# The folded weight of an mLSTM and feed-forward kernel by seven half-block products a row pair, its sums on GpSimd, and quarter products split in two

## The chip, the cores and the metric

One core of one Trainium2 chip. The metric is the device time of one launch in microseconds, as the median of several runs of the same kernel; the profile is one more execution, with the hardware profiler on. TensorE is called PE, VectorE DVE, ScalarE ACT, GpSimd POOL and SyncE SP, as the profile does.

## The reference

An mLSTM cell for 4 batches, 8 heads, 768 time steps and head width 40, then a feed-forward part whose two hidden products are multiplied. Cut to what matters here:

```python
# cell, for each time step t:
C = f_stab * C + i_stab * outer(v[t], k[t]);  n = f_stab * n + i_stab * k[t]
y[t] = sigmoid(o_gate[t]) * (C @ q[t]) / max(abs(n @ q[t]), 1)
# feed-forward: x is y with the 8 heads side by side, 3072 tokens x 320
a = x @ w1                  # 320 -> 1024
b = x @ w2                  # 320 -> 1024
h = a * b @ w3              # 1024 -> 1024
out = h @ w_out             # 1024 -> 320
```

All arrays are float32 (w1, w2, w3 and w_out arrive as float64 and are converted by the kernel). Since `(a * b @ w3) @ w_out` is `(a * b) @ (w3 @ w_out)`, the kernel computes the product `w3 @ w_out`, 1024 x 320, once and calls it w3o. This is "the fold".

## The kernel before, in words

**Blocks and steps.** The tokens are 24 blocks of 128 (6 stretches of time by 4 batches). A Python loop over s writes the whole program out, 32 steps long; nothing loops on the chip. Step s computes the cell of block s and finishes the output y of block s - 1 (`quarter_work`, from L338). Around the cell, each step has pieces of the feed-forward part:

- `up`: for 256 tokens and two of the eight blocks f of 128 hidden columns, the products x·w1 (tile pa) and x·w2 (pb). The 320 rows of x are two times 128 and a rest of 64; the rest is done by "quarter products" of 64 x 64 x 256, four of which share the array (`up_rest`, L631). `up_rest` then copies pa to a_sb on ACT (L638) and multiplies pb by a_sb on DVE into ab (L639). One up block runs in each of steps 2 to 5, two in each of steps 6 to 15.
- `fetch`, `scale_next`, `convert` (L211 to L251): a piece of a weight is read by SP, scaled on ACT (L191, L195) and turned into float32 on DVE (L199, L200). Pieces of w3 are also transposed on DVE, in squares of 32 (L248), into tiles w3T: two buffers, one for each row block ko of 128 of the 1024 rows. n_cvt says how many pieces step s converts; the reads run four pieces ahead.
- `fold`, `w3_mm` (L253 to L264): a row block whose w3T is ready costs eight products of 128 x 128 x 320 into a bank wp, one for each 128 of the 1024 inner terms (ki), which ACT then copies into w3o (L264). Two row blocks are folded in step 10, one in each of steps 11 to 16.
- `ffn_out` (L733): ab times w3o into a bank po, copied to o_sb on ACT (L741) and written out; from step 16.
- Steps 19 to 30 have `up_by_seven` and steps 27 to 31 `out_by_seven`, which do the same work on larger blocks by seven products of half blocks for eight (Strassen's scheme in Winograd's form), with the sums by `weight_sums`, `token_sums`, `out_weight_sums` and `ab_sums` on POOL and DVE.

**The cell on the engines.** PE: products of the weights and of the state (ph, pi), then of q and k (ss) and of the decayed v and k (pc). DVE: h (L423, L430), the masked product of the scores (L397), the state (L404, L414), the denominator (L438 to L441), the gated output (L443, L445), then the turned copies of k and q for the next step (L317, from step 9), and after them the converts. POOL: the decayed state (L335), which waits for L404; vw of the next block (L330); two masks (L308); and until step 16 a copy that doubles y's rest (L476).

**What sets the order.** Each engine works through its own list in the order in which the program writes the operations; PE's order is pinned by `in_order` (L84), and `issue_after` puts chosen operations behind others on the same list (the converts stand behind the turn of the next q and k, L967). Semaphores carry the rest. PE writes into four rotating banks of PSUM for px (y transposed), wp, pa, pb and po; the cell has four banks of its own. `x_trans` (L486) turns y of an earlier block to xT by PE and a copy on ACT.

Of the kernel before, what the change touches and what calls it, by code (L numbers as in the profile page):

```python
# [8 lines left out]
FP = mybir.dt.float32  # L9
# [7 lines left out]
def kernel(  # L17
# [59 lines left out]
    def mps(shape, name):  # L77
        pool = banks.pop(0)
        banks.append(pool)
        return pool.tile(shape, FP, name=name, tag="m")  # L80
# [10 lines left out]
    def mm(out, lhsT, rhs, start=True, stop=True):  # L91
        in_order(nc.tensor.matmul(out, lhsT=lhsT, rhs=rhs, start=start, stop=stop))  # L92
# [135 lines left out]


    w3T_t = {}  # L230
    turned_w3, ready_w3 = [], []

    def scale_next(early=False):
        scaled.append(pend.pop(0))
# [2 lines left out]
    def convert():  # L237
        if not scaled:
            scale_next()
        dst, raw, ko, half = scaled.pop(0)  # L240
        if dst is not None:
            to_f32(dst, raw)
            return
        w3 = wst.tile([128, CW], FP, name="w3", tag="w3")
        to_f32(w3, raw)
        if half == 0:
            w3T_t[ko] = wst.tile([128, FO, 128], FP, name="w3T", tag="w3T")
        nc.vector.transpose(out=w3T_t[ko].rearrange("c k (m r) -> c m k r", r=32)[:, 2 * half:2 * half + 2],  # L248
                            in_=w3.rearrange("r (m c k) -> r m k c", m=2, k=FO))
        if half:  # L250
            turned_w3.append(ko)  # L251

    def fold():  # L253
        while ready_w3:
            w3_mm(ready_w3.pop(0))
        ready_w3.extend(turned_w3)
        turned_w3.clear()

    def w3_mm(ko):
        w3T = w3T_t.pop(ko)  # L260
        wp = mps([128, DM], "wp")
        for ki in range(FO):
            mm(wp, w3T[:, ki, :], wo[:, ki, :], start=(ki == 0), stop=(ki == FO - 1))
        nc.scalar.mul(out=w3o[:, ko, :], in_=wp, mul=UP ** -2)  # L264


    qT_t, kT_t, vw_t, before_t, y_t, x_t = {}, {}, {}, {}, {}, {}
# [65 lines left out]
    def decayed(new, old, n, x):  # L333
        c, b = divmod(n, B)
        nc.gpsimd.tensor_tensor(out=new, in0=old, op=OP.mult, in1=decay[:, b * NP:(b + 1) * NP, 2 * c + x:2 * c + x + 1]  # L335
                                .to_broadcast([P, NP, D1]))
# [281 lines left out]
    def up(gr, fs, cs):  # L618


        if gr not in ab_t:
            ab_t[gr] = [ffn.tile([128, FO, 2 * P], FP, name="ab", tag="ab", bufs=6) for _ in range(2)]
        x, n = x_t[gr], cs.stop - cs.start
        pa, pb = mps([128, len(fs), n], "pa"), mps([128, len(fs), n], "pb")
        for p, wt in ((pa, w1), (pb, w2)):
            for i, f in enumerate(fs):
                for cc in range(KF):
                    mm(p[:, i, :], wt[:, cc, f * 128:(f + 1) * 128], x[:, cc, cs], start=(i == cc == 0), stop=False)
        return pa, pb, x, gr, fs, cs

    def up_rest(pa, pb, x, gr, fs, cs):  # L631
        for i, f in enumerate(fs):
            for j, e in quarters:
                mm((pa, pb)[j][halves[e], i, :], wr[halves[j], f * 128 + e * L:f * 128 + (e + 1) * L],
                   x[halves[j], KF, cs], start=False, stop=(i == len(fs) - 1))
        j, t0 = divmod(cs.start, 2 * P)
        a_sb = ffn.tile([128, len(fs), cs.stop - cs.start], FP, name="a_sb", tag="a_sb")
        nc.scalar.mul(out=a_sb, in_=pa, mul=UP ** -2)  # L638
        nc.vector.tensor_tensor(out=ab_t[gr][j][:, fs[0]:fs[-1] + 1, t0:t0 + a_sb.shape[-1]], in0=pb, in1=a_sb, op=OP.mult)  # L639

# [87 lines left out]

        return single, shared, left, product

    def ffn_out(blocks, pos=None):  # L733

        pos = pos or [mps([P, DM], "po") for _ in blocks]
        for (gr, j), po in zip(blocks, pos):
            for f in range(FO):
                mm(po, ab_t[gr][j // 2][:, f, j % 2 * P:(j % 2 + 1) * P], w3o[:, f, :], start=(f == 0), stop=(f == FO - 1))
        for (gr, j), po in zip(blocks, pos):
            o_sb = ffn.tile([P, DM], FP, name="o_sb", tag="o_sb", bufs=2)  # L740
            nc.scalar.copy(out=o_sb, in_=po)  # L741
            t0 = j * S + gr * P
            nc.scalar.dma_start(out=out[t0:t0 + P, :], in_=o_sb)


    KH, NH = FO // 2, DM // 2

    def out_weight_sums():

        T_o.extend(m[:, i * KH * NH:(i + 1) * KH * NH].rearrange("p (f n) -> p f n", n=NH)  # L750
                   for m, i in ((v_all, 0), (gates, 0), (gates, 1), (q_all, 0)))
        (B11, B12), (B21, B22) = ([w3o[:, k * KH:(k + 1) * KH, i * NH:(i + 1) * NH] for i in range(2)] for k in range(2))
        T1, T2, T3, T4 = T_o
        for dst, p, q in ((T1, B12, B11), (T2, B22, T1), (T3, B22, B12), (T4, B21, T2)):
            yield nc.gpsimd.tensor_tensor(out=dst, in0=p, in1=q, op=OP.subtract)

    T_o, S_o = [], {}
    wsums = out_weight_sums()

    def quarters_of_ab(gr, j):  # L760
        return [[ab_t[gr][j][:, k * KH:(k + 1) * KH, t * P:(t + 1) * P] for k in range(2)] for t in range(2)]
# [49 lines left out]
    n_out = [0] * 27 + [1, 0, 1, 0, 3]  # L811
    w12 = [("w12", i, part) for part in range(2) for i in range(2 * KF + 1)]
    todo = w12[5:] + [("wo", i, 0) for i in range(FO)] + [("w3", ko, part) for ko in range(FO) for part in range(2)]
    n_cvt = [0, 0, 2, 0, 1, 2, 3, 3, 3] + [2] * 6
    n_fetch = [5, 5, 10]
    pinned, ahead = 32, 9
    behind = ExitStack()
# [2 lines left out]
    for s in range(len(n_up)):  # L820
# [21 lines left out]
        if s < NU:  # L842
            if s >= B:
                decayed(state[s % B][1], state[s % B][0], s, 0)
        if s == 2 or N_DVE < s < NY + 2:
            twice(s - 2)
        if NY <= s - 2 < NU:
            get_back(s - 2)
        while s >= N_DVE and turned < min(s - 2, NY):
            x_trans(turned)  # L850
            turned += 1
        fold()
        if s >= len(n_up) - 2:
            ab_sums(*summed.pop(0))
        def pairs():
# [13 lines left out]
            seven[1]()  # L869
        if seven and s <= NU:  # L870
            ffn_out([downs.pop(0) for _ in range(n_down[s])], [cell[1][:, i, 0:DM] for i in range(2)])
        else:
            for _ in range(n_down[s]):
                ffn_out([downs.pop(0)])
# [2 lines left out]
        if seven and s > NU:  # L877
            seven[0]()
        now = [ups.pop(0) for _ in range(n_up[s])]
        open_ups = [up(*x) for x in now] if s != 2 else []  # L880
        if s == 3:
            turn(3)
        def rest():
            for x in open_ups:
                up_rest(*x)
            if seven:
                seven[2]()
            if s == 3:
                scale_next()
                scale_next()  # L890

        def between():
            twice(1)
            weighted(2)
            rows_of_u(3)
            for _ in range(3):
                scale_next()
            for n in range(2):
                x_trans(n)
                if n == 0:  # L900
                    warm(1, small=38)
            for _ in range(3):
                convert()
            turn(2)
            block = up(*now[0])
            weighted(3)
            weights(3)
            masks(3)
            out_gate(2)
            convert()  # L910
            up_rest(*block)

        gated = None
        if s <= NU:
            gated = quarter_work(s, rest, between if s == 2 else None, convert if s == 3 else None)
        else:
            rest()
        with tc.issue_after(gated.ins) if gated else nullcontext():
            if seven:
                seven[3]()  # L920
            for _ in range({NU: 1, NU + 1: 3}.get(s, 0)):
                next(wsums)
            if s == NU + 1:
                ab_sums(*summed.pop(0))
            if NY <= s - 2 < NU:
                x_turn(s - 2)
            for n in () if s == 1 else (s + 2,) if s < B else (s + 2, s + 3) if s == B else (s + 3,):
                if n < N_U:
                    rows_of_u(n)
            if N_DVE <= s + 1 < NU:  # L930
                gated = turn(s + 1)
            if s - 2 in range(4 * GT - 1, NU, GT):
                token_sums((s - 2) // GT)
            if s < len(n_up) - 2 and n_out[s + 1] and s > NU + 2:
                ab_sums(*summed.pop(0))
# [28 lines left out]
        if s == B:  # L964
            for i, r in enumerate(third):
                nc.sync.dma_start(out=U_d[i * GC:(i + 1) * GC].rearrange("c r t -> r c t"), in_=U3[r])
        with tc.issue_after(gated.ins) if N_DVE <= s + 1 < NU else nullcontext():  # L967
            for _ in range(n_cvt[s] if s < len(n_cvt) else 0):
                convert()
                converted += 1  # L970
# [9 lines left out]
            for ins in keep_order(front):  # L980
                behind.enter_context(tc.issue_after(ins))
    behind.close()
    assert not ups and not sevens and not downs and not outs and not summed and not todo and not pend and not turned_w3 and not ready_w3, (len(ups), len(downs), len(todo), len(pend))
# [1 line left out]
_INS = ['q', 'k', 'v', 'i_gate', 'f_gate', 'o_gate', 'moe_w1', 'moe_w2', 'moe_w3', 'moe_w_out']  # L985
_OUTS = [((3072, 320), 'float32')]
# [25 lines left out]
```

## Time and profile before

| what | value |
|---|---|
| runs of the kernel before | 426.22, 426.43, 430.01 us; median 426.43 |
| the profiled execution | 427.89 us, its span 425.8 us |
| granted PE clock, mean | 0.996 |
| PE busy | 414.1 us, 97% of the span |
| DVE busy | 313.5 us, 74% |
| POOL busy | 154.3 us, 36% |
| ACT busy | 150.1 us, 35% |
| DMA, share of the 16 engines in hardware queues | 53.9% and 2.7% |
| products of the fold (wp) | 128 records, 35.9 us busy |
| POOL, subtraction of 128 x 512 (L711) | 27.4 us in 22, 1268 ns each |
| POOL, subtraction of 128 x 640 (L755) | 4, of 1545 to 1995 ns |
| DVE, product ab of two PSUM and SBUF inputs (L639) | 16.4 us in 24, 688 ns each |

A row of the groups of instructions reads: line, engine, operation, output <- inputs, shapes, count, then busy time and mean of one, then the idle time of the engine just before them and what ended it. A float32 product is two records on PE (and two weight loads on PEld). Records overlap in PE's pipeline, so the mean of one is longer than the distance from one to the next. In the chain of waits, "issue" is time in which the engine waited for nothing that the profile shows.

### The profile page before, as it was taken

Reading aid. Unit: us, or ns where it says so; the run is one execution under the profiler, and the core shown is the slowest. Engines: PE = TensorE matmul, PEld = TensorE weight load, DVE = VectorE, ACT = ScalarE, POOL = GpSimd, SP = SyncE. Lnnn points to the kernel's source line nnn. Section 1 sums busy time; section 2 is a strip of 40 time slices with the busy share of each in tenths; the row PEclk is TensorE's granted clock in tenths of the full one; section 3 lists DMA queues with packets and bytes.
Section 4 is the critical chain, followed back from the end, with each engine's and each line's share of the span. In section 5 each row is a group of like instructions: output and inputs, shape, how many; then the busy total and the mean of one; then the engine's idle time right before and its main releaser. Section 6 shows DMA issues by size and latency. Waiting matters only on the chain.

```text
span 425.8 us, 13079 instructions
## 1 busy us (share of the span) xinstructions
PE 414.1 (97%) x5353; PEld 335.3 (79%) x5353; DVE 313.5 (74%) x635; ACT 150.1 (35%) x404; POOL 154.3 (36%) x211
## 2 busy tenths in 40 slices
PE   7989989999999999999999999999999999999996
PEld 4768878888688788787777778788778879888896
DVE  6676986888949779778736966596868699575971
ACT  4766865567723623630433313032311110210000
POOL 4421342233303303303307751546453587542100
PEclk9989999999999999999999999999999999999999
DMA  8999998598977776985425675756421120000001
GB/s 186 204 173 245 214 144 140 134 193 180 215 183 154 166 182 135 181 164 105 89 80 130 153 141 121 142 133 117 87 44 36 35 39 2 31 2 31 2 32 62
DMA packets 135211, 51.15 MB, mean 120 GB/s; under 512 B 109360, under 2 KB 126960, under 8 KB 135152
## 3 DMA queue, kind: packets, MB, share of 16 engines
q1 hardware_dynamic: 131552, 46.29, 53.9%
q10 hardware_dynamic: 3600, 4.03, 2.7%
q8 instruction: 42, 0.69, 0.7%
q14 instruction: 17, 0.14, 0.1%
HBM read 44.50 MB, written 5.80 MB: 118 GB/s over the span
## 4 chain that ended last, share of the span: by engine, by line
PE 53%; issue 20%; DVE 7%; POOL 7%; SPq 7%; DMA 5%; ACT 1%; POOLq 0%; DVEq 0%
PE cell L92 17%; PE pa L92 12%; PE o L92 8%; PE pb L92 8%; PE p L92 3%; POOL pw L308 3%; SPq L184 3%; DVE w3T L666 2%; PE pt L95 1%; POOL vw L330 1%; SPq L148 1%; DMA raw<-in_moe_w_dram 1%; PE fill L92 1%; POOL raw L659 1%; POOL state L335 1%
## 5 line engine op out<-in xcount | busy, mean ns | idle before, releaser
L335 POOL TENSOR_TENSOR state<-state,decay 128x164 f32<-128x164 f32 x40 | 20.0, 500 | 154.8 <-DVE state L404 129.0
L92 PE MATMUL pa<-xT,w 128*128 128x256 f32 x240 | 60.4, 382 | 0.0
L92 PEld LDWEIGHTS pa<-xT,w 128*128 128x128 f32 x240 | 44.4, 190 | 6.8 <-DVE h L430 0.4
L303 ACT ACTIVATE pw<-pw,aT 128x64 f32<-128x64 f32 x184 | 46.4, 339 | 3.2 <-ACT o_sb L741 1.9
L92 PE MATMUL pb<-xT,w 128*128 128x256 f32 x192 | 45.4, 379 | 0.0
L729 POOL TENSOR_TENSOR ab<-ab,a_sb 128x512 f32<-128x512 f32 x22 | 29.4, 1356 | 32.2 <-DVE ab L684 32.2
L92 PEld LDWEIGHTS pb<-xT,w 128*128 128x128 f32 x192 | 36.4, 190 | 5.0
L711 POOL TENSOR_TENSOR wo<-wo 128x512 f32<-128x512 f32 x22 | 27.4, 1268 | 29.8 <-DVE wo L686 29.8
L92 PE MATMUL pa<-xT,wr 64*64 64x256 f32 x384 | 37.0, 386 | 0.5 <-DVE wr L200 0.5
L92 PE MATMUL wp<-wo,w3T 128*128 128x320 f32 x128 | 35.9, 433 | 1.1 <-DVE ab L639 0.6
L308 POOL TENSOR_SCALAR_AFFINE_SELECT pw<-pw 64x512 f32<-64x512 f32 x48 | 35.8, 746 | 3.0 <-ACT pw L303 1.2
L92 PE MATMUL pb<-xT,wr 64*64 64x256 f32 x384 | 36.4, 380 | 0.0
L92 PE MATMUL cell<-w3o,ab 128*128 128x320 f32 x128 | 35.4, 432 | 0.0
L638 ACT ACTIVATE a_sb<-pa 128x512 f32<-128x512 f32 x24 | 14.3, 598 | 59.0 <-PE pb L92 59.0
L639 DVE TENSOR_TENSOR ab<-pb,a_sb 128x512 f32<-128x512 f32 x24 | 16.4, 688 | 23.2 <-ACT a_sb L638 22.8
L92 PEld LDWEIGHTS wp<-wo,w3T 128*128 128x128 f32 x128 | 23.8, 190 | 10.5 <-DVE ab L639 0.8
L92 PEld LDWEIGHTS cell<-w3o,ab 128*128 128x128 f32 x128 | 24.3, 190 | 9.5
L92 PEld LDWEIGHTS pa<-xT,wr 64*64 64x64 f32 x384 | 18.9, 132 | 15.4 <-issue 8.8
L686 DVE SCALAR_TENSOR_TENSOR a_sb<-pa,wo 128x512 f32<-128x512 f32 x12 | 8.3, 689 | 29.8 <-PE pa L92 29.8
L430 DVE TENSOR_TENSOR h<-cell,h 64x164 f32<-64x164 f32 x88 | 28.6, 326 | 1.6
L92 PE MATMUL po<-w3o,ab 128*128 128x320 f32 x96 | 26.4, 433 | 0.0
L92 PEld LDWEIGHTS po<-w3o,ab 128*128 128x128 f32 x96 | 18.1, 190 | 7.3
(180 smaller groups left out, 846.4 us busy)
## 6 DMA issues: line engine op xcount, KB each, us to landing
raw<-in_moe_w_dram SPq DMA_DIRECT2D x64, 128.0 KB, 3.4
kbuf<-in_k_dram SPq DMA_DIRECT2D x24, 160.0 KB, 4.5
v_all<-in_v_dram SPq DMA_DIRECT2D x24, 160.0 KB, 4.9
o_in<-in_o_gate_dram SPq DMA_DIRECT2D x24, 160.0 KB, 4.8
pw<-U_d SPq DMA_DIRECT2D x28, 128.0 KB, 3.5
raw<-in_moe_w_dram SPq DMA_DIRECT2D x5, 512.0 KB, 6.7
raw<-in_moe_w_out_dram SPq DMA_DIRECT2D x8, 320.0 KB, 4.1
gates<-in_k_dram SPq DMA_DIRECT2D x28, 80.0 KB, 2.5
```

The source lines that it names most:

```text
L92: in_order(nc.tensor.matmul(out, lhsT=lhsT, rhs=rhs, start=start, stop=stop))
L184: nc.sync.dma_start(out=dst, in_=src)
L303: nc.scalar.activation(out=pw[:, h, :], in_=src[:, h, :], func=AF.Exp, bias=aT[:, c, b * H + h:b * H + h + 1])
L308: nc.gpsimd.affine_select(out=pw[r], in_=pw[r], compare_op=OP.is_ge, fill=0.0, base=0, pattern=[[0, H], [1, L]], channel_multiplier=-1)
L335: nc.gpsimd.tensor_tensor(out=new, in0=old, op=OP.mult, in1=decay[:, b * NP:(b + 1) * NP, 2 * c + x:2 * c + x + 1] .to_broadcast([P, NP, D1]))
L430: nc.vector.tensor_tensor(out=part, in0=ph[x][halves[e]], in1=part, op=OP.add)
L638: nc.scalar.mul(out=a_sb, in_=pa, mul=UP ** -2)
L639: nc.vector.tensor_tensor(out=ab_t[gr][j][:, fs[0]:fs[-1] + 1, t0:t0 + a_sb.shape[-1]], in0=pb, in1=a_sb, op=OP.mult)
L666: nc.vector.tensor_tensor(out=dst, in0=p, in1=q, op=OP.subtract)
L686: nc.vector.scalar_tensor_tensor(out=out, in0=p, scalar=UP ** -2, in1=q, op0=OP.mult, op1=OP.add)
L711: aside_by.tensor_tensor(out=kept[j][:, 1:4:2], in0=kept[j][:, 1:3], in1=kept[j][:, 3:4].to_broadcast([128, 2, TH]), op=OP.add)
L729: aside_by.tensor_tensor(out=t[:, f:FO:FH, :], in0=t[:, f:FO:FH, :], in1=a, op=OP.mult)
```

## The change

1. **The fold.** The eight row blocks of w3 are taken as four row pairs (i). With A the 256 x 1024 pair, cut in 2 x 2 blocks (by row block and by half of the inner terms), and B = w_out cut in 2 x 2 (half of the inner terms, half of the 320 columns), the pair's 256 x 320 result takes seven products of half blocks instead of eight, each of four matmuls of 128 x 128 x 160: 28 of width 160 in place of 16 of width 320. Sums are S1 = A21 + A22, S2 = S1 - A11, S3 = A11 - A21, S4 = A12 - S2 and T1 = B12 - B11, T2 = B22 - T1, T3 = B22 - B12, T4 = B21 - T2.
   - `fold_first`: A11·B11 and A12·B21 into wp (8 matmuls), copied on ACT by `first_copy`. At the end of steps 9, 11, 13 and 14, behind the cell.
   - `fold_second`: A22·T4, S1·T1, S2·T2, S4·B22, S3·T3 into wq and wp (20 matmuls), copied on ACT to M2 and M1. In steps 10, 12 and 14 between the first up block (with its quarter products) and the second; in step 16 between the first six and the last two f of `ffn_out` (with the cell ahead of those last two).
   - its five adds (three of 160 columns, two of 320): on POOL behind the cell in steps 10, 12, 14, on DVE in step 16.
   - the T sums on POOL: T1 and T2 in step 8; T4 and T3 (in B12's place) in step 9, ahead of and behind the S sums. The S sums (four of 128 x 512) on POOL in steps 9, 11, 13, 15. S3 takes A21's place in w3T; B21 - T2 is formed once more in step 15 for the last pair, in B21's place, since the last pair's result takes the place in w3o where T4 lay.
   - memory: S and M in a spare ab tile or spare raw tiles; T in a new tile fold_m and in w3o; o_sb lives in fold_m; the w3 tile has one buffer for two.
2. **Two steps' piece counts.** n_cvt is 3 for 2 in step 5 and 2 for 3 in step 8: a piece of w_out comes a step earlier, and the fetches with it.
3. **Copies and products.** In steps 9, 11 and 13 both a_sb copies are written ahead of both products ab; in these steps `x_trans` stands at the end of the step.
4. **Split quarter products.** In steps 2, 3 and 4 (both f) and in step 6 (first up block, first f) a quarter product of 64 x 64 x 256 is written as two of 64 x 64 x 128.

The diff, cut to its core:

```diff
-    def w3_mm(ko):
-        w3T = w3T_t.pop(ko)
-        wp = mps([128, DM], "wp")
-        for ki in range(FO):
-            mm(wp, w3T[:, ki, :], wo[:, ki, :], start=(ki == 0), stop=(ki == FO - 1))
-        nc.scalar.mul(out=w3o[:, ko, :], in_=wp, mul=UP ** -2)
...
+    def fold_weight_sums():
+        (B11, B12), (B21, B22) = halves_of(wo)
+        T1, T2, T4 = (m.rearrange("p (f n) -> p f n", n=NH) for m in
+                      (fold_m[:, 0], fold_m[:, 1], w3o[:, FO - 2:FO].rearrange("p k n -> p (k n)")))
+        fold_T.extend((T1, T2, B12, T4))
+        for dst, p, q in ((T1, B12, B11), (T2, B22, T1), (T4, B21, T2), (B12, B22, B12)):
+            yield nc.gpsimd.tensor_tensor(out=dst, in0=p, in1=q, op=OP.subtract)
...
+    def fold_sums(i):
...
+        for dst, p, q, op in ((S1, A21, A22, OP.add), (S2, S1, A11, OP.subtract), (A21, A11, A21, OP.subtract),
+                              (S4, A12, S2, OP.subtract)):
+            nc.gpsimd.tensor_tensor(out=dst, in0=p, in1=q, op=op)
...
+    def fold_first(i):
+        A11, A12 = (w3T_t[2 * i][:, k * KH:(k + 1) * KH] for k in range(2))
+        (B11, _), (B21, _) = halves_of(wo)
+        wp = fold_products(((A11, B11), (A12, B21)))
+        return lambda: nc.scalar.mul(out=fold_of(i)[:, 0:3:2], in_=wp, mul=UP ** -2)
...
+    def fold_second(i):
...
+        for p, x, a, b, first, last in ((wq, 1, A22, T4, True, False), (wp, 0, S1, T1, True, False), (wp, 1, S2, T2, False, False),
+                                        (wq, 0, S4, B22, False, True), (wp, 2, S3, T3, False, True)):
+            for k in range(KH):
+                mm(p[:, x], a[:, k, :], b[:, k, :], start=(first and k == 0), stop=(last and k == KH - 1))
...
+        nc.scalar.mul(out=M2, in_=wq, mul=UP ** -2)
+        nc.scalar.mul(out=M1, in_=wp, mul=UP ** -2)
+        def adds(by=nc.gpsimd):
+            for out, p, q in ((C[:, 1], M1[:, 1], C[:, 0]), (C[:, 0], C[:, 0], C[:, 2]), (C[:, 2], M1[:, 2], C[:, 1]),
+                              (C[:, 1:4:2], C[:, 1:3], M1[:, 0:1].to_broadcast([128, 2, NH])), (C[:, 1:3], M2, C[:, 1:3])):
+                by.tensor_tensor(out=out, in0=p, in1=q, op=OP.add)
...
+    def up_rest(pa, pb, x, gr, fs, cs, split=(1, 1), later=None):
+            parts = split[i]
+            n = (cs.stop - cs.start) // parts
+            for t in range(parts):
+                for j, e in quarters:
+                    mm((pa, pb)[j][halves[e], i, t * n:(t + 1) * n], wr[halves[j], f * 128 + e * L:f * 128 + (e + 1) * L],
+                       x[halves[j], KF, cs.start + t * n:cs.start + (t + 1) * n], start=False,
+                       stop=(i == len(fs) - 1 and t == parts - 1))
...
-    n_cvt = [0, 0, 2, 0, 1, 2, 3, 3, 3] + [2] * 6
+    n_cvt = [0, 0, 2, 0, 1, 3, 3, 3, 2] + [2] * 6
...
+        elif s == 16:
+            finish = ffn_out([downs.pop(0) for _ in range(n_down[s])], split=FO - 2)
+            fold_second(FO // 2 - 1)(nc.vector)
...
+        if s in (10, 12, 14):
+            up_rest(*up(*now.pop(0)))
+            adds.append(fold_second((s - 10) // 2))
...
+            later = [] if s in (9, 11, 13) else None
+            for i, x in enumerate(open_ups):
+                up_rest(*x, split=(2 if s in (3, 4) or s == 6 and i == 0 else 1, 2 if s in (3, 4) else 1), later=later)
...
+        if s in (9, 11, 13):
+            x_trans(turned)
+            turned += 1
+        if s in (9, 11, 13, 14):
+            first_copy = fold_first((s - 8) // 2)
...
+            for _ in range({8: 2, 9: 1}.get(s, 0)):
+                next(fsums)
+            for x in adds:
+                x()
+            if s in (9, 11, 13, 15):
+                fold_sums((s - 9) // 2)
+            if s == 9:
+                next(fsums)
```

## The prediction

> **What bounds the kernel now.** I read the page first (engines, then the chain that ended last), then the costliest groups.
>
> ```profile
> PE 414.1 (97%) x5353; PEld 335.3 (79%) x5353; DVE 313.5 (74%) x635; ACT 150.1 (35%) x404; POOL 154.3 (36%) x211
> ...
> PE 53%; issue 20%; DVE 7%; POOL 7%; SPq 7%; DMA 5%; ACT 1%; POOLq 0%; DVEq 0%
> ...
> L92 PE MATMUL wp<-wo,w3T 128*128 128x320 f32 x128 | 35.9, 433 | 1.1 <-DVE ab L639 0.6
> ```
>
> TensorE is the bound: it is busy for 414.1 of 425.8 us, so a column taken from it is worth its time wherever nothing else is late. The wp row is the fold: 64 products, 128 records (two to a float32 product).
>
> Next the windows from cell end to cell end, over the steps in which the fold runs: steps 10, 11, 12 to 15, and 16 (start:end, length, then busy time of each engine).
>
> ```profile
> 107.30:127.70 20.40, 19.82 (x228) 15.39 (x228) 13.85 (x27) 9.43 (x23) 3.41 (x6) 1.00 0.86 196
> 127.70:142.95 15.25, 15.25 (x215) 12.33 (x212) 12.21 (x24) 6.46 (x18) 3.46 (x6) 1.00 0.79 170
> 142.95:204.00 61.05, 60.52 (x796) 48.70 (x792) 48.15 (x92) 22.95 (x62) 13.82 (x24) 1.00 0.73 147
> ```
>
> PE never waits for data in steps 11 to 15, but DVE has 12.0 to 12.2 us of work in a step of 15.25. A step is 0.4 (px) + 4.3 (one wp) + 6.9 (two up blocks) + 1.8 (their quarter products) + 1.8 (cell) = 15.2 us. Step 12 on DVE, from the timeline:
>
> ```profile
> 147.20 0.82 DVE L445 TENSOR_TENSOR y<-h,o_in 128x320 f32<-128x320 f32 x1
> 147.94 1.14 DVE L317 STREAM_TRANSPOSE kT<-gates 128x512 f32<-128x512 f32 x1
> ...
> 153.20 1.11 DVE L248 STREAM_TRANSPOSE w3T<-w 128x512 f32<-128x512 f32 x1
> 157.11 0.69 DVE L639 TENSOR_TENSOR ab<-pb,a_sb 128x512 f32<-128x512 f32 x1 [2.80 <-ACT a_sb L638]
> 157.97 0.69 DVE L639 TENSOR_TENSOR ab<-pb,a_sb 128x512 f32<-128x512 f32 x1 [0.17 <-ACT a_sb L638]
> ```
>
> The cell ended at 142.95; DVE is through its converts at 154.3, 11.35 us later, and idles 2.8 us until a_sb comes. That 2.8 us is all the room there is.
>
> The timeline on PE shows that it was short of instructions ("issue"), in the cells of step 4 and in step 12:
>
> ```profile
> 59.05 0.35 PE L92 MATMUL cell<-vw,kbuf 64*40 64x41 f32 x12 [1.49 <-issue]
> ...
> 144.57 3.12 PE L92 MATMUL wp<-wo,w3T 128*128 128x320 f32 x11 [0.54 <-issue]
> ```
>
> [...] L666 takes 418 ns alone and up to 1490 ns beside POOL's L659.
>
> ```profile
> L666 DVE TENSOR_TENSOR w3T<-xT x6: 418/780/1490, 238.2 to 354.5; 128x256 f32<-128x256 f32 x6
> ```
>
> [...] Queue q8 shows 42 packets; PE stalls at only three that I can place (57.57, 96.2, 144.0), each amid short matmuls. [...] 128x512 is 1.27 us on POOL (L711), 0.69 on DVE (L639, one input in PSUM).
>
> **The change part by part.** Matmuls of width 160 run in the output stage:
>
> ```profile
> 400.83 1.11 PE L92 MATMUL o<-v_all,pw 128*128 128x160 f32 x7
> 401.78 2.34 PE L92 MATMUL o<-gates,pw 128*128 128x160 f32 x16
> 403.96 0.30 PE L92 MATMUL o<-w3o,ab 128*128 128x160 f32 x1
> ```
>
> From 400.83 to 403.96 are 23 records: 0.136 us each, 0.272 a product. (Their mean of 299 ns is latency.)
>
> *Fold on PE.* Removed: 64 products of 0.539 (eight take 4.31) = 34.5 us. Added: 4 row pairs x 28 products x 0.272 = 30.4. **-4.1**, 1.0 a pair. A pair is 8 "first" products (2.2 us, end of steps 9, 11, 13, 14) and 20 "second" ones (5.4 us, in steps 10, 12, 14 between the two up blocks, in 16 amid ffn_out).
>
> *POOL, pair 0 (step 9).* POOL's new queue starts behind the state product L335, which ends 3.2 us after the cell (145.66 + 0.46 against 142.95). Behind it stand T4 (640 wide: 2.0, L755), S1 to S4 (4 x 1.27) and B12 (2.0): T4 ready at 5.2, S1 6.4, S2 7.7, S4 10.2, B12 12.2. PE: px 0.4, first 2.2, an up block 3.45 with quarters 0.9 bring second to 6.9; its five groups of 1.09 would end at 12.35. The last (S3·T3) waits for B12 at 12.2 and ends at 13.3. No overlap with DVE is priced here: **+1.2**, from 1.0 up to 3. Behind these POOL rows queue the vw and the masks of step 10 (0.7 + 2 x 0.75: at 14.5, due only at the cell, at 18.5): covered by 4 us. On DVE the first w3T transpose of step 9 now waits for S4 (its buffer): at 10.2 instead of 8. Behind it are a convert and step 10's first product; DVE is through at 14, and the next product due behind an up block is at 18: covered.
>
> *Odd steps 11 and 13.* These have lost their wp and are 0.4 + 6.9 + 1.8 + 1.8 = 10.9 us from cell to cell, yet the previous step's converts still end 11.35 after the cell. So the first product L639, whose PSUM bank "first" needs, ends at 12.05 instead of about 10.6. First would start at 10.9: it waits 1.15. The adds of step 10 or 12 (three of 160, two of 320, 3.1 us of POOL) can block L443 and L445 and make that 2.1. **+1.2 a step, +2.4 together.** What is late next: the second product (2.1 later than usual against the cell), then h (L423), the state (L404), POOL's S sums and the transposes that wait for S4. S4 is ready 2.1 + 3.2 + 5.1 = 10.4 after the cell; second reaches its S4 group at 1.15 + 2.2 + 0.4 + 4.35 + 3.3 = 11.4: covered by 1.0, and up to 1 a step if POOL starts 2 us later. The long even steps (18.5 us from cell to cell with first) absorb DVE's late converts.
>
> *Step 16.* The last pair's five adds are on DVE, and ffn_out's last two f need them. Copy M1 (about 0.75 after second's end, as L638 0.60 and its wait), then 3 x 0.25 + 2 x 0.49 = 1.75 on DVE: 2.5, against the cell's 1.8 between: **+0.8**, up to 1.3. The S sums of step 15 have no converts beside them and end 8.3 after the cell; needed at 10: covered.
>
> *Removed wait.* At 107.77 wp waited 0.58 for a product L639; the new first reads an earlier bank. **-0.5** (the T1, T2 sums of step 8, 4.0 us of POOL, can eat it: to 0).
>
> *Instruction blocks.* Splitting the quarter products in steps 2, 3, 4 and 6 keeps columns (group of four 64x256: 0.214 us; two of half width the same) and adds 28 x 4 = 112 instructions: nothing on PE by itself[...]. 96 of them stand before step 4's cell[...]: the 1.49 probably goes. [...] **-1.2**, between -2.3 (all three stalls gone) and +1 (new ones).
>
> *At nothing:* copies on ACT (four of 320 and four of 320 + 480 for eight of 320; ACT is 35% busy); one wo convert a step earlier, one w3 convert from step 8 to 7 and SP's reads with it (they are ahead of need by a step; a read that landed late would hold DVE and be a wait of its own length in an odd step); x_trans put at the end of steps 9, 11, 13 (px stays between the same neighbours for PE); the order "both copies, then both products", which moves nothing on ACT or DVE, as each engine keeps its order.
>
> Sum: -4.1 + 1.2 + 2.4 + 0.8 - 0.5 - 1.2 = **-1.4 us**. The profiled execution was 427.89 (span 425.8 and 2.1 around it): 426.5. The three runs' median lies 1.46 below that execution, so 426.43 - 1.4 = **425.0**.
>
> **Rivals.** *B, the waits are hidden:* if DVE gets its converts done 1.5 us sooner (the step's DVE work is 12.0, its order free within) and B12 is in time, only step 16 stays, and all fetch stalls go: -4.1 - 0.5 - 2.3 + 0.8 = -6.1, **420.3**. For it: DVE idles 2.8 us a step today. Against: the order puts the products behind the converts.
>
> *C, slower[...]:* POOL's rows stand back to back, 10.3 us in step 9, 5.1 in steps 11, 13, 15, 3.1 in 10, 12, 14[...]. Three of them blocked by 0.8 (L666's 1.49 less 0.42 is 1.07) put 2.4 more on each odd step, so 2 x 3.6; second waits 1 more for S4 in each (2); pair 0 costs 3, step 16 1.3: 13.5 - 4.1 - 0.5 = +8.9, **435**. It decides from 5.8 us of waits (break-even: 4.1 + 0.5 + 1.2). Against: stream transposes and PSUM-fed operations were not slowed beside POOL (L317 1.1 in both cases), and DVE has idle time in even steps.
>
> *D, it doesn't do what it says:* a product of 160 in the fold takes more than half of one of 320, the weight load (190 ns a record, L92 PEld) coming to the front. At 0.300 the fold saves 0.9: +1.8, **428.2**. Against: the output stage runs 23 in a row at 0.136 with the same loads.
>
> **How the numbers follow.** A 0.55, B 0.22, C 0.13, D 0.10. A's own range is 422.5 to 428.5. One per cent, 4.3 us, is about what a measurement of this kernel can tell: bounds 422.2 and 430.7. Faster: B and a little of A, 0.23. Slower: C and the top of A and D, 0.16. Same: 0.61. The range 420 to 430.5 leaves out most of C and the tail of B.
>
> **What would show it.** wp spacing 0.136; idle PE before S3·T3 in step 10, about 1 us, released by POOL; idle PE before first in steps 11 and 13, about 1.2, released by DVE's product; 0.8 before po in step 16; no issue wait near 57. Wrong if odd steps show no wait (toward B), or S sums hold up PE by more than 2 us a pair (toward C), or new issue waits appear.

## The result and the profile after

The changed kernel is slower: 430.99 us (median of 14 runs, 428.99 to 433.34) against 426.27 (14 runs of the kernel before, 424.28 to 430.01), ratio 1.0105 with a 95% interval of 1.0077 to 1.0132. The forecast was 425.0 with a range up to 430.5: a small gain was expected and a loss of 4.7 us came.

The profiled execution took 430.79 us, its span 429.1. First the page: engines, the chain that ended last, and a row of PE that has a new wait.

```profile
PE 410.1 (96%) x5505; PEld 340.9 (79%) x5505; DVE 327.2 (76%) x640; ACT 151.8 (35%) x408; POOL 200.6 (47%) x247
...
PE 73%; SPq 10%; DVE 8%; issue 3%; DMA 3%; POOL 1%; ACT 1%; DVEq 0%; POOLq 0%
...
L92 PE MATMUL po<-w3o,ab 128*128 128x320 f32 x96 | 26.7, 435 | 1.1 <-DVE w3o L325 1.1
```

PE's busy time did fall, by 4.0 us (414.1 to 410.1), while the span grew by 3.3. So the engine that sets the end now waits more. Not all of the 4.0 is the fold's: in the trace of before, PE ran at half its clock for 3.4 us in step 2 (23.41 to 26.83), which that of the changed kernel does not have, and there the stretch from cell 1 to cell 2 took 15.89 us for 14.13. DVE is 13.7 us busier although it got only five operations more, and these take 1.95 us: its operations got longer. The waits stand in PE's timeline, one line each:

```profile
109.12 2.44 PE L92 MATMUL wp<-wo,w3T 128*128 128x160 f32 x16 [1.82 <-DVE ab L710]
...
120.37 1.35 PE L92 MATMUL wq<-wo,ab 128*128 128x160 f32 x8 [0.87 <-POOL ab L284]
122.32 1.35 PE L92 MATMUL wp<-wo,w3T 128*128 128x160 f32 x8 [0.60 <-POOL wo L266]
...
142.51 2.44 PE L92 MATMUL wp<-wo,w3T 128*128 128x160 f32 x16 [1.19 <-DVE ab L710]
...
221.11 2.42 PE L92 MATMUL po<-w3o,ab 128*128 128x320 f32 x8 [1.06 <-DVE w3o L325]
```

A sixth, of 1.16 in step 13, has the same releaser as that at 142.51. Together they are 6.70 us. Beside the first of them, at 109.12, stands the wait of the kernel before at the same place:

```profile
108.35 8.88 PE L92 MATMUL wp<-wo,w3T 128*128 128x320 f32 x32 [0.58 <-DVE ab L639]
```

To see where time went I cut both traces at the end of each cell's last product (vw, kbuf). PE's idle time is "idle", the rest "work"; all in us, worked out from the records of PE.

| from cell to cell | before: length (idle) | after: length (idle) |
|---|---|---|
| start to 9 | 107.29 | 106.82 |
| 9 to 10 | 20.44 (0.58) | 23.05 (3.30) |
| 10 to 12 | 31.27 (0.54) | 31.38 (1.19) |
| 12 to 14 | 30.58 (0) | 31.36 (1.16) |
| 14 to 16 | 30.56 (0) | 27.45 (0) |
| 16 to 17 | 10.96 (0) | 14.29 (1.06) |
| 17 to PE's end | 191.49 | 191.47 |

Between the cells of steps 9 and 17: 123.81 before, 127.53 after, +3.7. Idle time went up by 5.6 (1.12 to 6.70), work down by 1.9 (122.7 to 120.8). With -0.5 ahead of step 9 this is the 3.2 us by which PE's last record ends later. The -0.5 is no gain of the change: it holds the 1.8 of the slower step 2 in the trace of before.

Why was first(0) (`fold_first` of row pair 0; second(0) is its `fold_second`) so late? The timeline of DVE in step 8 and up to step 9's first product ab, the kernel before, then the changed kernel:

```profile
98.35 0.76 DVE L443 SCALAR_TENSOR_TENSOR o_in<-o_in,den 128x320 f32<-128x320 f32 x1
99.15 0.49 DVE L445 TENSOR_TENSOR y<-h,o_in 128x320 f32<-128x320 f32 x1
100.28 0.62 DVE L199 TENSOR_SCALAR w<-raw 128x512 uint32<-128x512 uint32 x1 [0.63 <-ACT raw L191]
...
107.65 1.24 DVE L639 TENSOR_TENSOR ab<-pb,a_sb 128x512 f32<-128x512 f32 x2
```
```profile
99.40 1.58 DVE L508 SCALAR_TENSOR_TENSOR o_in<-o_in,den 128x320 f32<-128x320 f32 x1
101.02 1.72 DVE L510 TENSOR_TENSOR y<-h,o_in 128x320 f32<-128x320 f32 x1
102.66 0.96 DVE L199 TENSOR_SCALAR w<-raw 128x512 uint32<-128x512 uint32 x1
103.75 1.10 DVE L200 CUSTOM_DVE_ANT_0 w<-raw,w 128x1024 uint16<-128x1024 uint16 x1
...
108.42 1.25 DVE L710 TENSOR_TENSOR ab<-pb,a_sb 128x512 f32<-128x512 f32 x2
```

and POOL of the changed kernel at the same time:

```profile
99.08 1.55 POOL L266 TENSOR_TENSOR fold_m<-wo 128x640 f32<-128x640 f32 x1
100.71 1.68 POOL L266 TENSOR_TENSOR fold_m<-wo,fold_m 128x640 f32<-128x640 f32 x1
```

L508 (L443 before) ends 0.35 us behind T1, and L510 (L445) 0.35 us behind T2: each started beside a POOL row and ended after it. With POOL idle either takes 0.49 us in both traces. The 0.76 of L443 stands beside the end of vw on POOL (98.03 to 98.76) and ends 0.35 us behind that too. L508 and L510 take 0.8 and 1.2 longer than in the kernel before; L199 and L200 behind them, beside vw and the masks, 0.3 and 0.2 longer than in the kernel before (0.62 and 0.92): 2.6 us in all.

DVE also came 1.05 us later into this stretch (99.40 for 98.35 at L508): one of step 7's converts is now a piece of w3, with its transpose, in place of a piece of w_out (part 2 of the change). Against the two stand one convert less in step 8 (2.3) and a wait of 0.63 that is gone. So step 9's first product, which frees the bank for first(0), comes at 108.42 instead of 107.65, 0.8 later; and PE is ready for it 0.5 earlier, at 107.30 instead of 107.77. That makes 1.82 of 0.58.

### The profile page after: what moved, and what is told of

Read it like the earlier page. It is cut to its first block, busy times and chain, and to the rows that moved or that the text cites. A ratio compares the mean times of both kernels' runs of the same rounds, so it can differ in the third digit from the quotient of the medians.

```text
span 429.1 us, 13439 instructions
## 1 busy us (share of the span) xinstructions
PE 410.1 (96%) x5505; PEld 340.9 (79%) x5505; DVE 327.2 (76%) x640; ACT 151.8 (35%) x408; POOL 200.6 (47%) x247
## 4 chain that ended last, share of the span: by engine, by line
PE 73%; SPq 10%; DVE 8%; issue 3%; DMA 3%; POOL 1%; ACT 1%; DVEq 0%; POOLq 0%
PE cell L92 20%; PE pa L92 19%; PE pb L92 12%; PE o L92 8%; SPq L139 5%; PE p L92 4%; PE wp L92 4%; PE po L92 3%; SPq L184 2%; PE wq L92 2%; DVE w3T L742 2%; SPq L153 1%; DVE pw L859 1%; DMA wo<-in_moe_w_dram 1%; PE px L95 1%
## 5 line engine op out<-in xcount | busy, mean ns | idle before, releaser
L92 PE MATMUL pa<-xT,wr 64*64 64x256 f32 (+1 forms) x412 | 37.7, 372 | 0.6 <-DVE wr L200 0.6
L92 PE MATMUL pb<-xT,wr 64*64 64x256 f32 (+1 forms) x412 | 37.1, 366 | 0.0
L92 PEld LDWEIGHTS pa<-xT,wr 64*64 64x64 f32 x412 | 19.9, 132 | 15.6 <-issue 9.8
L92 PEld LDWEIGHTS pb<-xT,wr 64*64 64x64 f32 x412 | 21.1, 133 | 3.0
L395 POOL TENSOR_TENSOR vw<-v_all,wT 128x328 f32<-128x328 f32 x24 | 19.8, 825 | 5.2 <-DMA v_all<-in_v_dram 3.9
```

Source lines behind the costliest of these rows:

```text
L395: nc.gpsimd.tensor_tensor(out=vw_t[n], in0=vbuf[n % NBV], op=OP.mult, in1=wT[:, c, b * H:(b + 1) * H].unsqueeze(2).to_broadcast([P, H, D1]))
```

## The experiments

Each is compared with runs of the kernel before made beside it, whose medians lie between 425.67 and 426.17 (23 to 52 runs a set). My theory by then: the loss is waits, PE waiting for DVE and POOL around the fold; rivals are named with each run.

**1. Quarter products whole again.**

```diff
-                up_rest(*x, split=(2 if s in (3, 4) or s == 6 and i == 0 else 1, 2 if s in (3, 4) else 1), later=later)
+                up_rest(*x, later=later)
...
-            up_rest(*block, split=(2, 2))
+            up_rest(*block)
```

> The changed kernel with the quarter products of steps 2, 3, 4 and 6 whole again (no columns change). Theory (the added time is waits of 5.6 us between the cells of steps 9 and 17, less 1.9 us of TensorE work; the splits are neutral): 430 to 432 us, the same as the changed kernel, and the waits before step 9 sum to within 1 us of its 3.8 us. Rival 1 (the splits cost: step 4 of the changed kernel has 3.1 us of idle TensorE where before had 0.5): 428 to 429.5. Rival 2 (the splits save instruction waits, as the prediction had it): 432 to 433.5, with an instruction wait of 1 us or more in the cell of step 4 or 5.

430.44 us, ratio 1.0105 (1.0072 to 1.0138): the same as with the splits. The waits for instructions did not vanish, they moved: the changed kernel has 1.58 in the cell of step 4 and 0.74 in that of step 6; this one has 0.36 in the cell of step 5 and these two, in the px of step 13 and in the cell of step 19:

```profile
162.06 0.57 PE L95 MATMUL px<-ident,y 128*128 128x128 f32 x2 [1.76 <-issue]
...
266.13 0.27 PE L92 MATMUL cell<-vw,kbuf 64*40 64x41 f32 x3 [0.95 <-issue]
```

The waits of steps 2 to 9 sum to 1.6 and not to about 3.8, so that part of the expectation did not hold. (The trace is of the slowest run, 433.05.) The label "issue" says only that the profile shows no releaser. That these are waits for instructions follows from the DMA records: of the 36 waits over 0.2 us with this label in all thirteen traces, 34 end 1.1 to 1.7 us after a packet of 16 KB landed on the instruction queue q8. (In the changed kernel PE's 5505 products and 5505 weight loads are about 256 to each of the 43 packets of q8. The product that ends such a wait has 450, 1986, 3265 or 4545 records of products and loads ahead of it in the trace of before, and 1729 or 2497 in that of the changed kernel: each number is 193 or 194 over a multiple of 256.) The other two are the waits for T4 in runs 5 and 7.

**2. No sums and no adds.** The T, S and last-stage sums are left out and plain blocks of the weights stand in for them, so the folded weight is not w3 times w_out; PE's products and ACT's copies keep number and size.

```diff
-        for dst, p, q in ((T1, B12, B11), (T2, B22, T1), (T4, B21, T2), (B12, B22, B12)):
-            yield nc.gpsimd.tensor_tensor(out=dst, in0=p, in1=q, op=OP.subtract)
+        fold_T.extend((B11, B22, B12, B21))
...
-        fold_S[i] = S1, S2, A21, S4
+        fold_S[i] = A21, A22, A21, A22
...
-        nc.scalar.mul(out=M2, in_=wq, mul=UP ** -2)
+        nc.scalar.mul(out=C[:, 1:4:2], in_=wq, mul=UP ** -2)
```

> The changed kernel without any of the fold's sums and adds on GpSimd and VectorE: the 112 products run on plain blocks of the weights and the copies go straight to w3o, so the folded weight is not w3 times w_out. TensorE and ScalarE have the same work. Theory (first waits for VectorE's product because the odd steps got shorter than VectorE's chain[...]): the waits at S4 and S3T3 of step 10 (0.87 and 0.60) and the one of step 16 (1.06) go, that of first(0) (1.82) goes because two converts stand where there were three and nothing blocks VectorE, and those of steps 11 and 13 stay at 0.9 to 1.2 each: 431.0 - 1.5 - 0.8 - 1.8 = 426.9. Rival (the waits of steps 11 and 13 are made by GpSimd's adds blocking VectorE): these go too, 424.6. Rival (the waits are not what costs): 430 or more.

424.48 us, ratio 0.9950 (0.9928 to 0.9971): below the kernel before. Its trace is of its slowest run, 428.69; the extra time lies ahead of step 9 (110.68 us for 107.29), and between the cells of steps 9 and 17, 121.20 us, PE has its full clock. There first(0), S4, S3T3 and step 16 do not wait. Steps 11 and 13 still do, by half:

```profile
141.71 2.44 PE L92 MATMUL wp<-wo,w3T 128*128 128x160 f32 x16 [0.61 <-DVE ab L702]
```

So of 1.19 there, 0.58 goes with the sums and 0.61 stays with the order of DVE's list alone. Neither theory was right on that; the time came nearer to the rival's 424.6.

**3. One convert between the products.** The second w3 convert of steps 10 and 12 is put between the two products of steps 11 and 13.

```diff
+            for i, x in enumerate(later or ()):
+                ins = x()
+                if i == 0 and s in (11, 13):
+                    with tc.issue_after(ins.ins):
+                        convert()
```

> The changed kernel with one edit of order: the second w3 convert of steps 10 and 12 stands on VectorE between the two products of steps 11 and 13, in place of ahead of both. Theory (first waits only because the first product is queued behind the converts): the waits ahead of first in steps 11 and 13 (1.19 and 1.16) fall below 0.3 each, no new one over 0.5: 431.0 - 1.9 = 429.1. Rival (VectorE is short of time whatever the order, so the state and S4 come later and second waits for S4 in steps 12 and 14): 430.5 to 431.5. Rival (the wait is for something other than the product's bank): unchanged, 431.0.

428.85 us, ratio 1.0066 (1.0044 to 1.0088): 2.1 us under the changed kernel, as expected. First does not wait any more in steps 11 and 13. S4 is late by 0.30 in step 14, and in step 12 by about 0.26, which PE's records show as length and not as idle time (work of 19.22 us from cell 11 to cell 12, against 18.95 in run 11). The wait for first was the product's place in the list.

**4. Step 16 in another order.** Eight of ffn_out's products come first, then second with S4B22 last and M1 copied first, then four more of ffn_out, the cell, and the last four.

```diff
-            finish = ffn_out([downs.pop(0) for _ in range(n_down[s])], split=FO - 2)
-            fold_second(FO // 2 - 1)(nc.vector)
+            finish = ffn_out([downs.pop(0) for _ in range(n_down[s])], split=FO - 2, amid=lambda: fold_second(FO // 2 - 1)(nc.vector))
```

> The changed kernel with step 16 in another order: the last pair's second products stand 4 products of ffn_out earlier, S3T3 ahead of S4B22, M1 copied ahead of M2, so that 2.2 us of ffn_out and the cell lie between second and ffn_out's last two f. Theory: the wait of 1.06 for the adds on VectorE goes and none over 0.3 comes: 431.0 - 1.0 = 430.0. Rival (S4, ready at 214.7 in the changed kernel, is late for second now): the wait moves to S4 and the time stays at 431.

429.84 us, ratio 1.0086 (1.0059 to 1.0113). The 1.06 is gone (the stretch from cell 16 to 17 is 13.16 instead of 14.29), and S4 holds nothing up.

**5. T1, T2 and T4 on VectorE.**

```diff
-        for dst, p, q in ((T1, B12, B11), (T2, B22, T1), (T4, B21, T2), (B12, B22, B12)):
-            yield nc.gpsimd.tensor_tensor(out=dst, in0=p, in1=q, op=OP.subtract)
+        for by, dst, p, q in ((nc.vector, T1, B12, B11), (nc.vector, T2, B22, T1), (nc.vector, T4, B21, T2), (nc.gpsimd, B12, B22, B12)):
+            yield by.tensor_tensor(out=dst, in0=p, in1=q, op=OP.subtract)
```

> The changed kernel with the three sums T1, T2 and T4 on VectorE in place of GpSimd (same place in the program). Theory (in step 8 the two T sums on GpSimd blocked VectorE for 3.0 us: L508 0.8, L510 1.2, L199 and L200 1.0 longer than in the kernel before; made on VectorE they take about 2 x 0.9, as L510's 128x320 takes 0.49): the wait ahead of first(0), 1.82, falls to 0.5 to 0.9; with T4 off GpSimd the S sums and B12 come 1.6 us sooner and the waits at S4 and S3T3 (0.87, 0.60) go: 431.0 - 1.1 - 1.5 - 0.5 of refills = 427.9. Rival (VectorE is short of time in step 8 whoever makes the sums): first(0) still waits 1.6 or more, 429.2. Rival (S4 waits for the S sums themselves): the waits in step 10 stay, 429.9.

430.53 us, ratio 1.0117 (1.0068 to 1.0167): a miss. First(0) waited 1.12 instead of 1.82 and S4 and B12 were in time, but T4 was late: in step 9 it stands behind y, and POOL's S sums, which now start at once, stand beside all three and make them longer (L508 and L510 take 0.49 with POOL idle). On DVE:

```profile
112.23 1.34 DVE L508 SCALAR_TENSOR_TENSOR o_in<-o_in,den 128x320 f32<-128x320 f32 x1
113.61 1.47 DVE L510 TENSOR_TENSOR y<-h,o_in 128x320 f32<-128x320 f32 x1
115.00 1.89 DVE L266 TENSOR_TENSOR w3o<-wo,fold_m 128x640 f32<-128x640 f32 x1
```

T4 takes 1.89 where T1, in step 8 with no sum on POOL beside it, takes 0.82, and second(0) waits 2.10 for it. (The trace labels that wait "issue", but the product starts within 0.1 us of T4's end.)

**6. No adds.** M2 goes straight to w3o, so the folded weight lacks terms; all T and S sums are made.

```diff
-        nc.scalar.mul(out=M2, in_=wq, mul=UP ** -2)
+        nc.scalar.mul(out=C[:, 1:4:2], in_=wq, mul=UP ** -2)
...
-                by.tensor_tensor(out=out, in0=p, in1=q, op=OP.add)
```

> The changed kernel without the adds of the last stage (M2 goes straight to w3o), so the folded weight lacks terms; all T and S sums are made. Theory (the adds put GpSimd's vw and masks of steps 10 and 12 three us later, where they block the converts L199 and L200): the waits in steps 11 and 13 fall from 1.19 and 1.16 to about 0.6, as without any sums; that of step 16 goes; first(0), S4 and S3T3 as in the changed kernel: 431.0 - 1.2 - 1.1 = 428.7. Rival (the S sums of the odd steps do it): waits of 1.1 in steps 11 and 13 stay, 429.9.

428.01 us, ratio 1.0055 (1.0036 to 1.0073), near the 428.7 of the theory. Step 13 waits 0.64 and step 16 not at all; first(0) waits 1.83 as before. Step 11 does not wait in this trace because step 10 was longer: PE's clock had fallen (below), and so this run can't say how much of step 11's wait the adds make; step 13's says 0.52 of 1.16. In the changed kernel the adds themselves do not lengthen L508 and L510 of step 10 (0.56 and 0.70; 0.76 and 0.82 without adds); vw and the masks, pushed behind the adds, fall on L199 and L200 (0.74 and 1.10 for 0.42 and 0.69).

**7. Cures 3 (for steps 9, 11 and 13), 4 and 5 together.**

> The changed kernel with the three cures together: T1, T2 and T4 on VectorE; one convert of steps 8, 10 and 12 between the two products of steps 9, 11 and 13; step 16 in the order of the run po16. Theory: none of the six waits between the cells of steps 9 and 17 stays above 0.4, so 6.7 us of waits and about 1 us of refills go: 431.0 - 7.5 = 423.5, below the kernel before by 2.4. Rival (waits move on to the next thing, S4 or the state, as VectorE does the same work): 426 to 428.

429.62 us, ratio 1.0083 (1.0059 to 1.0108): a miss for the reason of run 5. With first(0) in time, second(0) comes sooner and waits 3.85 us for T4, which takes 1.88 there, and then PE runs at half its clock. Windows right behind it, start:end, busy times, then PEclk in the third column from the right:

```profile
116.00:120.00 4.00, 4.00 (x15) 4.00 (x16) 3.84 (x4) 0.00 (x0) 4.00 (x4) 0.50 0.20 55
120.00:124.00 4.00, 4.00 (x25) 4.00 (x24) 3.61 (x5) 0.44 (x1) 1.92 (x4) 0.78 0.51 140
```

The stretch from cell 9 to cell 10 has 21.8 us of work where run 2 has 18.95: 2.8 us more.

**8. The kernel before with the splits alone.** The edit is the change's part 4.

> The kernel before with only the split quarter products of steps 2, 3, 4 and 6. Prediction as put on record: the instruction wait of 1.49 in the cell of step 4 goes, about -1.2: 424.7. Rival (a wait for instructions only moves to another place, as the run nosplit showed from the other side): 425.3 to 426.5, with instruction waits of 1 us or more in sum elsewhere.

429.18 us, ratio 1.0063 (1.0038 to 1.0088): the splits alone make the kernel before 3.4 us slower in the median, which neither side expected. Its trace has the forecast gain (the stretch from cell 4 to 5 is 7.54 for 9.28), a loss of 1.0 each in steps 4 and 6, and in step 12 a new wait with a lowered clock behind it:

```profile
159.09 0.28 PE L92 MATMUL cell<-vw,kbuf 64*40 64x41 f32 x7 [1.65 <-issue]
```
```profile
159.10:163.00 3.90, 3.90 (x17) 2.67 (x17) 3.06 (x9) 2.19 (x5) 2.36 (x4) 0.57 0.57 118
163.00:167.00 4.00, 4.00 (x18) 3.05 (x17) 3.93 (x6) 0.44 (x1) 1.09 (x3) 0.99 0.43 103
```

The stretches from cell 11 to 12 and 12 to 13 are 1.2 and 1.7 us longer. Up to the cell of step 9 this trace is 0.8 us ahead of that of before, and from there to the cell of step 17 it loses 3.2 (127.0 for 123.8). So the cost of the splits lies far behind them; that the other runs lose it at the same place is not shown.

**9. T4 in step 8 too.**

```diff
-            for _ in range({8: 2, 9: 1}.get(s, 0)):
+            for _ in range({8: 3}.get(s, 0)):
```

> As the run mend1, with T4 made on VectorE in step 8 beside T1 and T2, so that it stands behind nothing in step 9 (in mend1 it was blocked by the S sums until 115.9, second(0) waited 3.85 us and the clock fell to half for the next four). Theory (the waits between the cells of steps 9 and 17 are what makes the changed kernel slow): no wait over 0.4 there, no lowered clock; the stretch from the cell of step 9 to that of step 17 is 29.9 + 29.9 + 29.9 + 40.6 - 10.98 of overlap, about 119.5 us against 123.8 in the kernel before: 424.0 or less, if no wait for instructions of over 1.5 us comes in. Rival (a wait for instructions and the lowered clock behind it take the gain back): 425 to 428, with such a wait in the profile.

425.55 us, ratio 0.9996 (0.9971 to 1.0021): 5.4 under the changed kernel, level with the kernel before, and not at the 424.0 of the theory: cell 9 to cell 17 takes 122.95 us and not 119.5. S4 (1.03) and B12 (0.33) still hold second(0), and S4 holds steps 12 and 14 (0.28, 0.32).

**10. Run 9 with whole quarter products.**

> mend2 with the quarter products whole. Theory [...]: the same time as mend2 but for the waits for instructions, which move: each one of over 1.5 us that stands in the profile of one and not of the other is worth 1.5 to 3.4 us, the larger where the clock falls behind it. Rival (the splits are free and gainful as such): mend2n slower than mend2 by 1.5 us with a wait of 1.5 in the cell of step 4.

427.79 us, ratio 1.0034 (1.0006 to 1.0061): 2.2 more. The splits help here. Without them waits for instructions stand at 59.20 (1.75), 97.08 (0.72), 140.20 (0.62), 161.06 (1.39, with 1.9 us of lowered clock behind it) and 264.68 (1.33); with them only at 69.66 (0.74). Its one profile is of its slowest run, 431.64.

**11. All four T sums on VectorE in step 8, and S4B22 last in every pair.**

```diff
-        for by, dst, p, q in ((nc.vector, T1, B12, B11), (nc.vector, T2, B22, T1), (nc.vector, T4, B21, T2), (nc.gpsimd, B12, B22, B12)):
+        for by, dst, p, q in ((nc.vector, T1, B12, B11), (nc.vector, T2, B22, T1), (nc.vector, T4, B21, T2), (nc.vector, B12, B22, B12)):
...
-                                        *(tail if i < 3 else tail[::-1])):
+                                        *tail[::-1]):
...
-            for _ in range({8: 3}.get(s, 0)):
+            for _ in range({8: 4}.get(s, 0)):
```

> As the run mend2, with all four T sums on VectorE in step 8 and S4B22 as the last group of second in every pair (M1 copied ahead of M2). Theory: the waits for S4 and B12 left in mend2 (1.03 and 0.33 in step 10, 0.28 and 0.32 in steps 12 and 14) go with their refills (0.8, 0.26, 0.26), and 0.83 more of VectorE in step 8 still leaves first(0) without a wait over 0.4: 425.6 - 2.5 = 423.1, under the kernel before by 0.7 per cent. Rival (VectorE's 3.3 us of sums in step 8 make first(0) wait again): 425 to 426, with a wait of 1 us there. Rival (a longer S4 last holds up the second up block's bank behind the copy M2): a new wait at pb in steps 10, 12 and 14.

424.32 us (18 runs) against 425.67, ratio 0.9966 (0.9943 to 0.9989): under both kernels, and 1.2 over the 423.1 of the theory. One wait of the six is left, first(0) with 0.61; no new one at pb. Windows from cell to cell, over steps 10, 11, 12, 13 with 14, 15 with 16, and 17:

```profile
105.90:126.35 20.45, 19.71 (x252) 16.88 (x253) 18.34 (x30) 11.10 (x29) 9.23 (x10) 1.00 0.78 176
126.35:137.30 10.95, 10.95 (x196) 9.29 (x197) 10.24 (x21) 3.87 (x10) 7.43 (x11) 1.00 0.79 160
137.30:156.25 18.95, 18.95 (x253) 16.75 (x253) 16.81 (x27) 9.71 (x26) 9.33 (x10) 1.00 0.70 172
156.25:186.25 30.00, 30.00 (x448) 26.10 (x447) 27.05 (x47) 13.73 (x36) 16.74 (x21) 1.00 0.83 172
186.25:214.00 27.75, 27.65 (x410) 23.66 (x407) 23.50 (x45) 6.86 (x21) 17.91 (x22) 1.00 0.51 108
214.00:227.15 13.15, 13.15 (x172) 9.61 (x172) 6.47 (x16) 5.45 (x19) 7.86 (x9) 1.00 0.55 116
```

From step 12 on PE is busy to the end of each window (0.1 us idle in all), where the changed kernel lost 3.4. Cell 9 to cell 17 is 121.25 us, 2.6 under the kernel before. Its two edits were not run apart, and parts 2 and 3 of the change (the piece counts, the order of copies and products) were never run alone.

## Why the prediction was wrong, point by point

- **The step that failed: "Removed wait ... -0.5", with the bound "can eat it: to 0".** The new first does not read an earlier bank in effect: it waits for step 9's first product as wp did. That product comes 0.8 later and PE 0.5 earlier, so 1.82 stands where 0.58 had been, +1.2. The T sums of step 8 could not only eat a gain: they hold DVE for 2.1 us, and the rows that they push behind them for 0.5 more, in a step in which it has no room. The w3 convert moved from step 8 to step 7, which stood "at nothing", gives back 1.05 of the 2.3 that it saves in step 8. Of the 4.6 us between the forecast's -1.4 and the trace's +3.2 this step is 1.7, the largest part. Shown: without the sums the wait is gone (run 2).
- **The fold on PE, -4.1: too large.** Without a wait a pair's products take 7.71 us (2.17 for first's 8, 5.54 for second's 20: 0.275 each; step 12 of run 11) instead of 7.6, +0.4 for four pairs. An even step has two runs of quarter products with a change to them and back: 1.11 and 1.00 there, against 1.87 for the single run of step 10 before, 0.24 more a step and +0.7 in all. Against these, the 122.7 of before holds 0.4 of stops (19.86 in step 10 for 15.29 + 4.31, 15.45 in step 12 for 15.29). Without waits the stretch of work would be 119.4 (18.95 three times, 10.98 twice, 13.2, 14.24, 13.16: each the shortest in some trace) against 122.7: -3.3. Rival D had the sign of this and a size far too large (0.300).
- **A wait costs more than its idle time: not priced.** Work in the changed kernel is 120.8, not 119.4: 19.75 for 18.95 in step 10, 19.21 for 18.95 in steps 12 and 14, 13.24 for 13.16. That is 1.4 us at six waits. PE's records overlap (one of width 160 in the fold lasts 0.30 us and the next comes 0.14 behind it), so the start of a wait can be hidden in the end of the record ahead of it: in step 12 of run 3, 0.26 is lost with 0.01 of idle time. Whether that is all of it is not shown.
- **Pair 0, +1.2:** 0.87 + 0.60 = 1.47. The prediction had only B12 late, and its own times give 0.95 for it (13.3 less 12.35); here S4 made the larger part. The sums before B12 were 1.3 to 1.6 us each beside DVE instead of 1.27. That the total is near is in part luck: second came later because first(0) had waited. In run 9, with first(0) in time and T4 off POOL's list, S4 and B12 still cost 1.36.
- **Odd steps, +2.4:** 1.19 + 1.16 = 2.35. The size is right by luck: the forecast had all of it from the order of DVE's list. The order alone makes 0.61 a step (run 2), and the rest goes with the sums on POOL, which the forecast held for the upper end. With the convert moved the whole wait is gone (run 3).
- **Step 16, +0.8:** 1.06, of the kind forecast; a DVE sum of 160 took 0.33 and not 0.25, with gaps of 0.03 between. Run 4 removes it.
- **Instruction blocks, -1.2:** about -0.4 in this pair of traces. The waits labelled "issue" sum to 2.73 us before (0.41, 1.49, 0.30, 0.54) and to 2.32 in the changed kernel (1.58, 0.74). The 1.49 (it stands in the cell of step 5; the prediction, and the expectation of run 8, called it step 4) did go, and 1.58 and 0.74 came in its place; the 0.54 of step 12 went. As a part by itself it was misjudged: the splits cost the kernel before 3.4 us, give the mended one of run 9 2.2, and are neutral in the changed one. That 96 instructions more ahead of it would take the 1.49 away was the author's estimate.
- **Sum of the trace:** -3.3 + 1.4 + 5.6 (6.7 of waits less the 1.1 that went) - 0.5 = +3.2. The medians differ by 4.7. The 1.5 between is the profiled execution of before: it was 1.6 above its median, and the half clock in step 2 cost it about 1.8. In how many of the other runs that stands is not known.
- **Rival C** named what decided (DVE operations made longer beside POOL's rows, three on an odd step by its estimate, with waits above 5.8 us) and overpriced it at 435: the waits summed to 6.7 and not to 13.5. It had 0.13, too little: the place where DVE had least room, step 8 with its converts, was only in a bracket of my ledger. What it said of operations fed from PSUM holds: in the trace of before L684 of 128x512 took 0.68 to 0.69 us with POOL idle and beside POOL. **Rival B** (the waits are hidden) fell with the same 6.7.

## What to carry to other kernels

When PE's work is cut by moving sums to GpSimd, price them twice: by their own time and by what they do to VectorE. In the changed kernel L508 and L510 took 0.49 us with GpSimd idle and up to 1.59 and 1.72 beside its rows, the converts L199 (128x512) 0.43 and up to 0.96 and L200 (128x1024) 0.69 and up to 1.57; L760 (128x512), with one input in PSUM, took 0.68 to 0.69 in both cases. Two 128x640 sums held VectorE for 2.1 us when GpSimd made them, and took 1.65 us when VectorE made them itself. Removing work from a step also shortens the time that other engines had. Look at which engine's list now reaches past the step's end, and at the order in that list: moving one convert behind the product that PE needs, in two steps, was worth 2.1 us. The split of the quarter products, which adds 112 instructions and no columns, cost 3.4 us in the kernel before and gained 2.2 in that of run 9 (runs 8 and 10). So a comparison of two versions needs to look first for waits for instructions and for stretches of lowered clock, which one trace may have and the other not.

## What was not expected of the hardware

An idle stretch of PE of 1.4 to 1.8 us was in some traces followed by half the clock, which costs another 1.4 to 1.9 us. In the traces' clock records each such stretch is 3.41 us long at 0.50 (6.83 in run 7), and the changes of the clock in one trace lie whole multiples of 3.41 us apart. The mean granted clock is the third number from the right of a window's line. The kernel without adds, idle for 1.83 us ahead of this window:

```profile
106.70:110.00 3.30, 3.25 (x12) 3.25 (x13) 3.19 (x10) 1.01 (x4) 0.00 (x0) 0.52 0.78 205
```

The changed kernel, idle for 1.82 at nearly the same place in the program:

```profile
109.10:113.00 3.90, 3.88 (x24) 3.70 (x25) 3.47 (x11) 2.39 (x7) 0.35 (x1) 1.00 0.83 196
```

It followed idle times of 1.83, 1.76, 1.65, 1.56 and 1.39 (runs 6, 1, 8, 2 and 10) and did not follow others, among them 1.82 or 1.83 (the changed kernel, runs 3 and 4), 1.75 (run 10) or 2.10 (run 5). In steps 1 and 2 it followed idle times of only 1.0 to 1.2, in the trace of before and in runs 1, 3, 5, 7 and 8; in the other seven traces, which have a wait of that length there too, no drop came.

How the idle time falls on a grid of 3.41 us through the clock's changes does not decide alone. In run 6 all of the 1.83 lies in the stretch of the grid ahead of the drop (103.40 to 106.81); in run 3 all of its 1.83 lies in one too (107.32 to 110.74), and no drop came. PE was busy for 1.58 us in both, in run 6 with 87 records, most of them the cell's tiny products, in run 3 with 13 of full-size tiles. That this difference decides was not tested. Such drops may be a good part of the spread of 4 us between runs of one kernel; that is not shown either.
